# Making ten of the 56 feed-forward gelu tiles straight from PSUM, with a new table of who computes which softmax tile

## The chip, the cores and the metric

The kernel runs on one core of a Trainium2 chip. The metric is device time in microseconds (us) of one execution, the median of several. TensorE is called PE here, VectorE DVE, ScalarE ACT, GpSimd POOL and SyncE SP, as in the profile.

## The reference, cut to what matters

The input `x` is normalised once, and two branches read the result: attention with 32 query heads over one shared key and value head, and a feed-forward layer with a tanh-approximated gelu. The sum of `x` and both is the output.

```python
xn = layernorm(x)                      # x: 1 x 2048 x 512, bfloat16
q = (xn @ wq) as 32 heads of 16;  k = xn @ wk;  v = xn @ wv      # one k and v for all heads
p = softmax(q k^T / 4);  attn = (p v) as 2048 x 512 @ wo
h = gelu(xn @ w1 + b1)                 # w1: 512 x 1792
out = x + attn + h @ w2 + b2
```

## The kernel before, in words

**Softmax tiles.** Scores are computed transposed, keys on the partitions. A tile is 128 keys by 512 queries of one head. There are 2,048 tiles (4 blocks of 512 tokens, 8 groups of 4 heads, 16 key tiles, 4 heads) in 683 units of three. `scores(u)` writes the three tiles of unit `u` into banks 0 to 2 of PSUM when `u` is even and 3 to 5 when it is odd, so a unit's scores can start only once the unit two before it has been read. Bank 6 collects the probability-times-value sums (the pv matmuls), and bank 7 (`pM`, the side bank) serves everything else, one result at a time.

**Two ways for the exponential.** A tile's exponential is computed either by ACT (`exp`, into the buffer `E`, one pv matmul follows) or by DVE with an integer approximation: `p1` reads the bank and writes an int16 tile into `Dt`, `close_batch` makes three shifted copies of it and at last shifts the first tile itself, and five pv matmuls add up the five versions. DVE makes the copies; the last shift, called the in-place step below (line 1139 of the profile), is planned for POOL, but DVE takes it where the planner finds DVE free earlier. The string `DTAB` has one character a unit and says which of its tiles go to DVE: `.` none, `0` or `o` the first, `2` or `t` the third, `a` the first two, `x` or `X` all three (the letters `o t A B X` also close a batch of copies).

**Side work.** Projections of q, the feed-forward tiles and the output are cut into small jobs that are placed at units by tables (`QK`, `HP`, `YP`). `h_mm(tb, ft)` makes one feed-forward tile: 128 of the 1,792 hidden features for the 512 tokens of block `tb`. It issues 16 column-tiled matmuls (`mm4`, four for each quarter of the 512 inputs) into `pM`, and DVE adds the bias `b1T` and writes bfloat16 into `ubs[tb % 2]`: `ub` for the even blocks, and the no longer needed `x_sb` for the odd ones. There are 14 such tiles a block, 56 in all.

**Gelu batches.** Gelu needs another function table on ACT than exp does. So the gelus of two blocks are done together: `GU` places one batch after unit 182 (blocks 0 and 1) and one after unit 512 (blocks 2 and 3). `gelu` issues four activations a batch, each over `FG` = 7 tiles, in place in SBUF. While ACT is at them, DVE works on units whose three tiles are all its own. Later the y jobs multiply the gelu'd tiles by `w2`.

**Order.** `Prog.schedule` is a planner in the kernel: it simulates the five engines with costs written in the code and fixes each engine's order of instructions; `emit` adds the semaphore waits. On PE, scores come first, then the rest by due time. `op.sdeps` are dependencies for the planner, `op.rel` a release mark, and `allow` how long after becoming ready a step may wait.

Of the kernel before, what the change touches and what calls it, by code (L numbers as in the profile page):

```python
# [6 lines left out]
ACT = mybir.ActivationFunctionType  # L7
# [25 lines left out]
EV_ALLOW = -2.0  # L33
# [25 lines left out]
DMASK = {".": (), "0": (0,), "2": (2,), "a": (0, 1), "b": (1, 2), "x": (0, 1, 2),  # L59
         "o": (0,), "t": (2,), "A": (0, 1), "B": (1, 2), "X": (0, 1, 2)}  # L60
CLOSE = "otABX"
DTAB = "000to.2t0000t...t0t0..ooo0.o202t2.t..22t2.2t00.t2.0ot2.22o0002..0.o0o.2t22o2o0.00o.o.t.0o2tt.2.2t2o.2o2.20t0.00t22t.222o.2.2o.02.t2o0o.20ooot2.t0o0.t.o0.0t22t.ot.02oo2.2o.t022t0.2000oxXXXot...ooo2tt.202o0t0.t22t.0t2t.22t2ot.2.0oot2o.000.t0ot.20t.to0t02t0o.ot20oo0.20t2o0o..0o.o20o202.0t2t.2.t00oo..2oo020tt.020.t0o0.2.to.222t20o..t000t.2o.ttt22.2too.t.02ot20.t2.o0t0t2o.o0.t002020o..tt220o0.o2o.2t.22tt.o0.02t0oto0.00t.to2t.2.2tt0002t00o.t00.2t22..2o.00otot..2tt2t.t202..o.00t0.o.02o0.ot0t.2t00.tt2t220.0o00o22.2txXxtottot2o.t00t.2tt.ot22oo.tt.ot0.ooot002.to2o.t22o02.oo0o.2oo2t.220oo000.oo02.t.002o002o20.2t22o2t..2o.tttt0tt.2o.00t0t.0o0200t.t22tt00.2tt0.0o20t.0ttot0.2.ot2t..0o.0.."
YF = 664
Y_ALLOW = 2.0
H_ALLOW = 1.0
# [31 lines left out]
H_PRO = ()  # L97
# [6 lines left out]
TBW = 512  # L104
# [473 lines left out]
def bass_parallel_sum__grouped_kv_mqa__dense_activation_gelu__prompt_kernel(  # L578
# [21 lines left out]
    FT = F // P  # L600
    NTB = S // TBW
# [10 lines left out]
    with ExitStack() as es:  # L612
# [5 lines left out]
        ubs = (ub, x_sb)  # L618
# [15 lines left out]
        b1T = sb([P, FT], f32, "b1T")  # L634
# [51 lines left out]
        pO, pM = bank(6), bank(7)  # L686
        pr = Prog(nc)
# [3 lines left out]
        def B(b):  # L691
            return ("bank", b)
# [6 lines left out]
        def act(fn, r=(), w=(), n=TBW, allow=0.0, lat=0.22, **kw):  # L699
            return add("act", fn, r, w, occ=0.051 + n / 1.2e3, lat=lat, allow=allow, **kw)  # L700
# [17 lines left out]
        M4 = [(("bank", 7), j) for j in range(4)]  # L718
# [28 lines left out]
        def setup(fn, r=(), w=(), occ=0.16, due=0.0, lat=0.1, **kw):  # L747
# [31 lines left out]
              r=["mrow"], w=["isc"], due=10.0)  # L779
# [10 lines left out]
        for gl in range(2):  # L790
# [5 lines left out]
                    n=1500, due=0.01)  # L796
# [70 lines left out]
        def tr(a, b):  # L867
            return [("xnT", ti) for ti in range(a, b)]
# [375 lines left out]
        def ukey(tb, f):  # L1244
            return ("x", f) if tb % 2 else ("u", 0, f)

        def h_mm(tb, ft, ev=EV_ALLOW):
            for d in range(DT):
                mm4(pM, w1_sb[:, d, ft * P:(ft + 1) * P], xnT[:, d, tb * TBW:(tb + 1) * TBW], d == 0, d == DT - 1,
                   r=["w1"] + tr(4 * tb, 4 * tb + 4), w=[B(7)], allow=H_ALLOW if tb < NTB - 1 else 1.5)  # L1250
            dve(lambda e: e.tensor_scalar(ubs[tb % 2][:, ft, :], pM, b1T[:, ft:ft + 1], None, ALU.add),  # L1251
                r=["b1T"], w=M4 + [ukey(tb, ft)], n=TBW + 57, allow=ev)

        gelu_after = {}

        def gelu(tbs, u):
            parts = [(tb, f0) for tb in tbs for f0 in range(0, FT, FG)]
            hold = exps[u - 3:u + 1]
            for n, (tb, f0) in enumerate(parts):
                uu = ubs[tb % 2][:, f0:f0 + FG, :]  # L1260
                uk = [ukey(tb, f) for f in range(f0, min(FT, f0 + FG))]
                load = 1.35 * (n == 0) + 1.35 * (n == len(parts) - 1)
                o = act(lambda e, uu=uu: e.activation(uu, uu, ACT.Gelu_apprx_tanh), r=uk, w=uk, n=len(uk) * TBW + 1200 * load + 40,
                        kind="gelu", due=0.0, after=hold)
# [192 lines left out]
```

## Time and profile before

| | |
|---|---|
| median of 3 runs | 746.38 us (745.35 to 746.84) |
| the profiled execution | 746.57 us, span of its instructions 744.8 us |
| busy | PE 730.0, DVE 731.1, ACT 729.7, POOL 383.1 us |
| ACT, exps | 676 instructions, 680.5 us |
| ACT, gelu batches | 209.7 to 224.7 and 553.1 to 568.2 us, table loads included |
| DVE, h evacuations | 56 of 738 ns |
| granted TensorE clock, mean | 0.998 |

Records of one engine overlap, since an instruction starts before the one ahead has left the engine's pipeline; so sums of durations exceed the time they fill, and the step from one start to the next is the better price. PE's busy time is modelled and tells little. A group's line names the line, the engine, the operation, output and input tiles with their shapes, then busy us, mean ns of one, and the idle time before it with what ended it.

### The profile page before, as it was taken

How to read it: one execution, taken by the hardware profiler on the slowest of the kernel's cores; microseconds unless marked ns; L12 is line 12 of the kernel's file. 1: busy time of each engine (PE TensorE's matmuls, PEld its weight loads, DVE VectorE, ACT ScalarE, POOL GpSimd, SP SyncE). 2: the span in 40 equal slices, each digit the busy share in tenths (PEclk: the TensorE clock that was granted, in tenths of full speed). 3: DMA queues.
4: the chain of work that ended last, by engine and by line, in shares of the span. 5: the costliest groups of instructions: out<-in, count | busy, mean ns of one | idle time of the engine just before them, and what ended most of it. 6: DMA issues, size and time to landing. Idle time of an engine off the chain costs nothing.

```text
span 744.8 us, 22099 instructions
## 1 busy us (share of the span) xinstructions
PE 730.0 (98%) x9040; PEld 215.0 (29%) x9042; DVE 731.1 (98%) x1412; ACT 729.7 (98%) x741; POOL 383.1 (51%) x548
## 2 busy tenths in 40 slices
PE   7999999999999999999999999999998999999998
PEld 4322222222232222222222222222232222222223
DVE  7999999999999999999999999999999999999996
ACT  8899999999999999999999999999999999999995
POOL 7434555545533546545656455343543646546560
PEclk9999999999999999999999999999999999999999
DMA  9200100000011010100101110100100101010011
GB/s 310 66 19 17 30 11 19 22 11 16 16 46 30 13 35 18 24 16 16 32 7 26 26 38 18 37 16 15 24 12 24 31 17 38 16 46 17 10 31 37
DMA packets 31198, 23.34 MB, mean 31 GB/s; under 512 B 16385, under 2 KB 25722, under 8 KB 31098
## 3 DMA queue, kind: packets, MB, share of 16 engines
q1 hardware_dynamic: 31098, 21.94, 11.2%
q8 instruction: 72, 1.18, 0.7%
q14 instruction: 28, 0.23, 0.1%
HBM read 13.08 MB, written 2.35 MB: 21 GB/s over the span
## 4 chain that ended last, share of the span: by engine, by line
ACT 62%; PE 22%; DVE 13%; DMA 1%; SPq 1%; issue 1%
ACT E L1065 62%; PE pAll L1109 10%; PE pAll L1042 6%; DVE Dt L1096 6%; PE pAll L714 5%; DVE Dt L1143 5%; DMA b1row<-in_B_b_dram 1%; SPq L721 1%; DVE Of L1155 1%; PE pAll L708 0%; PE pAll L1418 0%; DVE Dt L1139 0%; DVE x_sb L1251 0%; DVE xnT L864 0%; DVE qp L1223 0%
## 5 line engine op out<-in xcount | busy, mean ns | idle before, releaser
L1065 ACT ACTIVATE E<-pAll 128x1024 bf16<-128x1024 f32 (+1 forms) x676 | 680.5, 1285 | 1.6 <-PE pAll L1042 1.5
L1139 POOL TENSOR_SCALAR Dt<-Dt 128x512 int16<-128x512 int16 x454 | 342.3, 754 | 325.9 <-DVE Dt L1143 116.0
L1109 PE MATMUL pAll<-Dt,V 128*32 128x512 bf16 x2775 | 409.4, 386 | 2.6 <-DVE Of L1155 2.3
L1096 DVE TENSOR_SCALAR Dt<-pAll 128x512 int16<-128x512 f32 (+1 forms) x541 | 367.6, 693 | 1.9 <-PE pAll L1042 1.0
L1109 PE MATMUL pAll<-E,V 128*32 128x512 bf16 x1493 | 303.9, 384 | 0.2 <-DVE Of L1155 0.2
L1143 DVE TENSOR_SCALAR Dt<-Dt 128x1024 int16<-128x1024 int16 (+6 forms) x540 | 288.0, 559 | 0.4
L1042 PE MATMUL pAll<-QT,KT 32*128 32x512 bf16 x2048 | 267.4, 385 | 4.5 <-ACT E L1065 2.4
L1042 PEld LDWEIGHTS pAll<-QT,KT 32*128 32x128 bf16 x2048 | 66.8, 91 | 295.3 <-ACT E L1065 283.8
L1109 PEld LDWEIGHTS pAll<-Dt,V 128*32 128x32 bf16 x2775 | 103.3, 95 | 102.5 <-issue 69.6
L1109 PEld LDWEIGHTS pAll<-E,V 128*32 128x32 bf16 x1493 | 72.9, 95 | 44.0 <-issue 33.0
L714 PE MATMUL pAll<-xnT,w_sb 128*32 128x512 bf16 x896 | 84.9, 384 | 0.0
L714 PE MATMUL pAll<-w_sb,x_sb 128*32 128x512 bf16 x448 | 76.4, 384 | 0.0
L714 PE MATMUL pAll<-w_sb,ub 128*32 128x512 bf16 x448 | 64.3, 383 | 0.1
L714 PE MATMUL pAll<-wop,oTp 128*32 128x512 bf16 x256 | 51.9, 383 | 0.0
L1186 POOL TENSOR_TENSOR oTp<-OfP,rbP 128x256 bf16<-128x256 f32 (+1 forms) x28 | 22.5, 809 | 14.6 <-DVE Dt L1143 7.9
L714 PEld LDWEIGHTS pAll<-xnT,w_sb 128*32 128x32 bf16 x896 | 21.4, 95 | 26.6 <-issue 16.8
L714 PE MATMUL pAll<-xnT,wq_sb 128*32 128x512 bf16 x256 | 26.8, 383 | 0.0
L1139 DVE TENSOR_SCALAR Dt<-Dt 128x512 int16<-128x512 int16 x101 | 26.2, 279 | 0.0
L1155 DVE COPY Of<-pAll 128x512 f32<-128x512 f32 x31 | 21.1, 680 | 0.1
L714 PEld LDWEIGHTS pAll<-w_sb,x_sb 128*32 128x32 bf16 x448 | 18.3, 95 | 8.2 <-issue 6.7
L1251 DVE TENSOR_SCALAR ub<-pAll,b1T 128x512 bf16<-128x512 f32 x28 | 20.7, 738 | 0.0
L1251 DVE TENSOR_SCALAR x_sb<-pAll,b1T 128x512 bf16<-128x512 f32 x28 | 20.7, 738 | 0.0
(125 smaller groups left out, 264.5 us busy)
## 6 DMA issues: line engine op xcount, KB each, us to landing
OfP<-Of SPq DMA_DIRECT2D x124, 32.0 KB, 2.0
rbP<-rden_rows SPq DMA_DIRECT2D x124, 32.0 KB, 1.8
w_sb<-in_B_w_dram SPq DMA_DIRECT2D x2, 1792.0 KB, 11.4
x_sb<-in_A_x_dram SPq DMA_DIRECT2D x18, 128.0 KB, 2.3
QT<-qp SPq DMA_DIRECT2D x124, 16.0 KB, 1.8
x_sb<-in_A_x_dram SPq DMA_DIRECT2D x7, 256.0 KB, 3.9
out_dram<-x_sb SPq DMA_DIRECT2D x12, 128.0 KB, 1.9
wq_sb<-in_A_wq_dram SPq DMA_DIRECT2D x1, 512.0 KB, 5.9
```

Source lines behind the costliest of these rows:

```text
L714: add("pe", lambda e, c=c, j=j: e.matmul(o[c, :], l[:, c], rh, start=start, stop=stop, tile_position=(0, 32 * j)), r, [(k, j) for k in w] ...
L721: return add(eng, lambda e: e.dma_start(o, i), r, w, dma=stream, occ=occ, lat=lat, allow=allow, **kw)
L1042: ins = e.matmul(o, l, rh, start=True, stop=True, tile_position=(q0, 0))
L1065: o = act(lambda e: e.activation(E[:, s0:s0 + na, :], bank(b0, na).rearrange("p (a n) -> p a n", a=na), ACT.Exp, scale=LN2 / 128.0), w=[B( ...
L1096: op = dve(lambda e: e.tensor_scalar(Dt[:, s:s + n, :], bank(bk, n).rearrange("p (a n) -> p a n", a=n), float(127 * 128) + SPL_D, SPL_MIN, ...
L1109: add("pe", lambda e, a, b: e.matmul(pO[32 * j:32 * j + 32, :], V1[:, v, kt, :], rhs, start=a, stop=b, tile_position=(0, 32 * j)), r=r + [ ...
L1139: add("pool", lambda e, d=d, k=k: e.tensor_scalar(d, d, 1.0, float(k), ALU.mult, ALU.add), [], [(("D", base[o > 0] + q), o)], occ=PL_OCC, ...
L1143: dve(lambda e, d=view(o, nb), q=view(i, nb), k=k: e.tensor_scalar(d, q, float(k), None, ALU.add), r=keys(i), w=keys(o), n=nb * n * TBW, m ...
L1155: dve(lambda e: e.tensor_copy(Of[:, i, :], pO), w=["O", ("Of", i)], allow=0.0)
L1186: "pool", lambda e, c=c: e.tensor_tensor(oTp[0:n, sl, c], OfP[0:n, s, c], rbP[0:n, s, c], ALU.mult),
L1251: dve(lambda e: e.tensor_scalar(ubs[tb % 2][:, ft, :], pM, b1T[:, ft:ft + 1], None, ALU.add), r=["b1T"], w=M4 + [ukey(tb, ft)], n=TBW + 57 ...
```

## The change

Of the 14 h tiles of the odd block of each batch, the last five (`GM` = 5, tiles 9 to 13) are no longer made ahead by `h_mm`. They are made during the gelu batch: 16 matmuls into `pM`, and then ACT reads the bank itself, adds the bias as the activation's per-partition bias, applies gelu and writes SBUF. These are called directs below. The other 23 tiles of the batch are done in six parts (`GCH` = 6) of 4, 4, 3, 3, 5 and 4 tiles, and a direct stands between each two parts. `DTAB` is another string, with 554 tiles for DVE instead of 555; `GU`, `HP` and the other tables stay.

```diff
-DTAB = (683 characters)
+DTAB = (683 others)
+GM = 5
+GCH = 6
...
+        def h_proj(tb, ft, al):
             for d in range(DT):
                 mm4(pM, w1_sb[:, d, ft * P:(ft + 1) * P], xnT[:, d, tb * TBW:(tb + 1) * TBW], d == 0, d == DT - 1,
-                   r=["w1"] + tr(4 * tb, 4 * tb + 4), w=[B(7)], allow=H_ALLOW if tb < NTB - 1 else 1.5)
+                   r=["w1"] + tr(4 * tb, 4 * tb + 4), w=[B(7)], allow=al)
+
+        def h_mm(tb, ft, ev=EV_ALLOW):
+            h_proj(tb, ft, H_ALLOW if tb < NTB - 1 else 1.5)
             dve(lambda e: e.tensor_scalar(ubs[tb % 2][:, ft, :], pM, b1T[:, ft:ft + 1], None, ALU.add),
...
         def gelu(tbs, u):
-            parts = [(tb, f0) for tb in tbs for f0 in range(0, FT, FG)]
+            te, to = tbs
+            n0 = round(GCH * FT / (2 * FT - GM)) if GM else 2
+            parts = []
+            for tb, n, k in ((te, FT, n0), (to, FT - GM, (GCH if GM else 4) - n0)):
+                f = 0
+                for i in range(k):
+                    m = -(-(n - f) // (k - i))
+                    parts.append((tb, f, m))
+                    f += m
+            seq = []
+            direct = list(range(FT - GM, FT))
+            for p in parts:
+                seq.append(p)
+                if direct:
+                    seq.append((to, direct.pop(0), 0))
+            seq += [(to, f, 0) for f in direct]
             hold = exps[u - 3:u + 1]
...
+            for n, (tb, f0, m) in enumerate(seq):
+                load = 1.35 * (n == 0) + 1.35 * (n == len(seq) - 1)
+                if m:
+                    uu = ubs[tb % 2][:, f0:f0 + m, :]
+                    uk = [ukey(tb, f) for f in range(f0, f0 + m)]
+                    o = act(lambda e, uu=uu: e.activation(uu, uu, ACT.Gelu_apprx_tanh), r=uk, w=uk, n=m * TBW + 1200 * load + 40,
+                            kind="gelu", due=0.0, after=hold)
+                else:
+                    n0_ = len(pr.ops)
+                    h_proj(tb, f0, H_ALLOW)
+                    for op in pr.ops[n0_:]:
+                        op.sdeps.append((exps[u - 3], True))
+                        op.rel = exps[u - 3]
+                    o = act(lambda e, tb=tb, f0=f0: e.activation(ubs[tb % 2][:, f0, :], pM, ACT.Gelu_apprx_tanh, bias=b1T[:, f0:f0 + 1]),
+                            r=["b1T"], w=M4 + [ukey(tb, f0)], n=TBW + 1200 * load, kind="gelu", due=0.0, after=hold)
                 hold = [o]
...
-                if tb > 0 or ft not in [h[0] for h in H_PRO]:
+                if (tb > 0 or ft not in [h[0] for h in H_PRO]) and not (tb % 2 and ft >= FT - GM):
                     at(HP[tb][ft], lambda tb=tb, ft=ft: h_mm(tb, ft), 0.66)
```

On ACT, at the first batch, the order before was this (`E<-pAll` is an exp, `ub<-ub` and `x_sb<-x_sb` a gelu part):

```order
L1065 ACTIVATE E<-pAll 128x1024 x5
L1263 ACT_TABLE_LOAD
L1263 ACTIVATE ub<-ub 128x3584 x2
L1263 ACTIVATE x_sb<-x_sb 128x3584 x2
L1065 ACT_TABLE_LOAD
L1065 ACTIVATE E<-pAll 128x1024 x2
L1065 ACTIVATE E<-pAll 128x1536 x3
```

And it is now, from the last exp ahead of the batch to the batch's fifth direct (`x_sb<-pAll,b1T`):

```order
L1067 ACTIVATE E<-pAll 128x512
L1284 ACT_TABLE_LOAD
L1284 ACTIVATE ub<-ub 128x2048
L1292 ACTIVATE x_sb<-pAll,b1T 128x512
L1284 ACTIVATE ub<-ub 128x2048
L1292 ACTIVATE x_sb<-pAll,b1T 128x512
L1284 ACTIVATE ub<-ub 128x1536
L1292 ACTIVATE x_sb<-pAll,b1T 128x512
L1284 ACTIVATE ub<-ub 128x1536
L1292 ACTIVATE x_sb<-pAll,b1T 128x512
L1284 ACTIVATE x_sb<-x_sb 128x2560
L1292 ACTIVATE x_sb<-pAll,b1T 128x512
```

Four long activations have become eleven, five of which read a bank that PE fills within the batch.

On PE, in the first batch, the order before was this, with the semaphores that a row waits for (`QT,KT` are scores, `Dt,V` pv matmuls on DVE's tiles, `xnT,w_sb` an h tile, `xnT,zeros` fillers):

```order
L1042 MATMUL pAll<-QT,KT 128x512 [waits tk_dve]
L1042 MATMUL pAll<-QT,KT 128x512 x2
L1109 MATMUL pAll<-Dt,V 32x512 x3
L714 MATMUL pAll<-xnT,w_sb 32x512 [waits tk_dve]
L714 MATMUL pAll<-xnT,w_sb 32x512 x15
L1418 MATMUL pAll<-xnT,zeros 32x512 x12
L1109 MATMUL pAll<-Dt,V 32x512 [waits tk_dve]
L1109 MATMUL pAll<-Dt,V 32x512 x10
```

And it is now, with the matmuls of the second and of the third direct in the first and last two rows:

```order
L716 MATMUL pAll<-xnT,w_sb 32x512 [waits tk_act]
L716 MATMUL pAll<-xnT,w_sb 32x512 x15
L1111 MATMUL pAll<-Dt,V 32x512 [waits tk_dve]
L1111 MATMUL pAll<-Dt,V 32x512 x3
L1447 MATMUL pAll<-xnT,zeros 32x512 x4
L1044 MATMUL pAll<-QT,KT 128x512 [waits tk_dve]
L1044 MATMUL pAll<-QT,KT 128x512 x2
L1111 MATMUL pAll<-Dt,V 32x512 x3
L716 MATMUL pAll<-xnT,w_sb 32x512 [waits tk_act]
L716 MATMUL pAll<-xnT,w_sb 32x512 x15
```

An h tile's matmuls now wait for ACT to have read the bank, and between two of them PE has rows that wait for DVE.

In the whole program, by counting rows of the order: exps 678 for 676 (534 of two tiles for 535, 141 of three as before, 3 of one); pv matmuls on DVE's tiles 2,770 for 2,775; DVE's part of the in-place steps 125 for 101; output normalisations on DVE (line 1186 before) 7 for 4. Behind the batches, ACT's first two exps are those of units 183 and 188 (187 and 188 before), and of 515 and 518 (516 and 517 before).

More of the change, by code (lines that the diff above doesn't have):

```diff
@@ L61 @@
 CLOSE = "otABX"
-DTAB = "000to.2t0000t...t0t0..ooo0.o202t2.t..22t2.2t00.t2.0ot2.22o0002..0.o0o.2t22o2o0.00o.o.t.0o2tt.2.2t2o.2o2.20t0.00t22t.222o.2.2o.02.t2o0o.20ooot2.t0o0.t.o0.0t22t.ot.02oo2.2o.t022t0.2000oxXXXot...ooo2tt.202o0t0.t22t.0t2t.22t2ot.2.0oot2o.000.t0ot.20t.to0t02t0o.ot20oo0.20t2o0o..0o.o20o202.0t2t.2.t00oo..2oo020tt.020.t0o0.2.to.222t20o..t000t.2o.ttt22.2too.t.02ot20.t2.o0t0t2o.o0.t002020o..tt220o0.o2o.2t.22tt.o0.02t0oto0.00t.to2t.2.2tt0002t00o.t00.2t22..2o.00otot..2tt2t.t202..o.00t0.o.02o0.ot0t.2t00.tt2t220.0o00o22.2txXxtottot2o.t00t.2tt.ot22oo.tt.ot0.ooot002.to2o.t22o02.oo0o.2oo2t.220oo000.oo02.t.002o002o20.2t22o2t..2o.tttt0tt.2o.00t0t.0o0200t.t22tt00.2tt0.0o20t.0ttot0.2.ot2t..0o.0.."
+DTAB = "02oto.0o20tt.t..0t0t..to.t022o.02o.o.oo.o.t0o0.22t.00ott22..t2t.00ot00.0t.2o2o2tt2t..t2.20t20.t.2o2o.0022.t.2220t000.tt.2o2.o20.22o.2t.t0t200o0t..o20.o00o2o0.t222022.t.0o20220t202.t.a2xoXoott2o2.0o.t0t.otto2tt2tt22.020t.0o.00oot.2oo..o0t022to22..2.o0t22to0.ot022tot.o022t0..t002o2.0t02tt.220.o.t0.02o2t002..0o0t.20t2t.2o.00t.t0.22t.0t2ot.02o0...t0t0t..ot2tt2o2oo.t2t.2o.o02o220t2t.20.o200oo0.o2..ooo20o..t2o.t2t0oo.2ot22t22.t.2t2202t.too00020200t.2....2tttt0to.o.2t2..t2t2.002o0oo.t2.220.0.tto.02o2t0o22202t002t.oxXaXot.20oo0o.oo2t.2t.22.tB.2ototoo0t2.t0220...tt02o200tt.t.o2.o22t2o.2t0t0222o0t..t20o2.2to00to0.o22t2..tt20o22.tt2t.0o22o2.t22.tt22t2ot.too00..o.oto.2t0o0o2t.o.ot.t0..."
 YF = 664
@@ L1245, in ukey @@
             return ("x", f) if tb % 2 else ("u", 0, f)
-        def h_mm(tb, ft, ev=EV_ALLOW):
+        def h_proj(tb, ft, al):
             for d in range(DT):
                 mm4(pM, w1_sb[:, d, ft * P:(ft + 1) * P], xnT[:, d, tb * TBW:(tb + 1) * TBW], d == 0, d == DT - 1,
-                   r=["w1"] + tr(4 * tb, 4 * tb + 4), w=[B(7)], allow=H_ALLOW if tb < NTB - 1 else 1.5)
+                   r=["w1"] + tr(4 * tb, 4 * tb + 4), w=[B(7)], allow=al)
+        def h_mm(tb, ft, ev=EV_ALLOW):
+            h_proj(tb, ft, H_ALLOW if tb < NTB - 1 else 1.5)
             dve(lambda e: e.tensor_scalar(ubs[tb % 2][:, ft, :], pM, b1T[:, ft:ft + 1], None, ALU.add),
@@ L1256, in gelu @@
         def gelu(tbs, u):
-            parts = [(tb, f0) for tb in tbs for f0 in range(0, FT, FG)]
-            hold = exps[u - 3:u + 1]
[L1259 to L1264, printed above, removed]
+            te, to = tbs
[14 more added lines that the diff above has]
+            seq += [(to, f, 0) for f in direct]
+            hold = exps[u - 3:u + 1]
+            for n, (tb, f0, m) in enumerate(seq):
[13 more added lines that the diff above has]
+                            r=["b1T"], w=M4 + [ukey(tb, f0)], n=TBW + 1200 * load, kind="gelu", due=0.0, after=hold)
                 hold = [o]
```

## The prediction

> **What bounds the kernel now.** I read first the page's span and busy times, then a table of stages that I cut at the two gelu batches, then the list of waits.
>
> ```profile
> span 744.8 us, 22099 instructions
> PE 730.0 (98%) x9040; PEld 215.0 (29%) x9042; DVE 731.1 (98%) x1412; ACT 729.7 (98%) x741; POOL 383.1 (51%) x548
> ```
>
> Three engines read 98%, so the shares alone say nothing. The table of stages (the columns are PE, PEld, DVE, ACT, POOL busy with instruction counts, then TensorE clock) separates them:
>
> ```profile
> 24.00:209.00 185.00, 183.14 (x2223) 52.05 (x2220) 184.21 (x338) 185.00 (x183) 96.42 (x132) 1.00 0.08 18
> 209.00:228.00 19.00, 18.85 (x257) 7.05 (x259) 18.96 (x26) 18.62 (x10) 6.03 (x9) 1.00 0.17 45
> 228.00:551.00 323.00, 321.47 (x4018) 90.78 (x4014) 322.34 (x626) 323.00 (x322) 166.33 (x218) 1.00 0.09 23
> 551.00:573.00 22.00, 19.13 (x228) 7.03 (x220) 21.51 (x32) 20.90 (x13) 9.29 (x14) 0.92 0.07 16
> 573.00:735.00 162.00, 160.96 (x2072) 44.45 (x2064) 160.65 (x332) 162.00 (x164) 90.00 (x114) 1.00 0.11 25
> ```
>
> In the three long stages ACT is busy for all of 185, 323 and 162 us: it never stops. It falls short only in the two short stages that hold the batches, by 0.38 and 1.10 us. The waits say who waits for whom:
>
> ```profile
> PEld pAll L1042 <- ACT E L1065: 283.8, 656, 0.8
> PEld pAll L1042 <- DVE Dt L1096: 8.0, 18, 0.7
> ACT E L1065 <- PE pAll L1042: 1.5, 3, 1.0
> ```
>
> The scores of a unit wait for ACT's exp 656 times of 683, for DVE's part 18 times; ACT waits for scores three times. ACT sets the pace, so what counts is work put on ACT, and gaps between its instructions.
>
> How full is ACT inside those stages? Its records overlap, so I need start-to-start steps. These are the two exp forms and the gelu parts, then one clean run of ten exps (one of 3 tiles, then nine of 2), then ACT around the batches:
>
> ```profile
> L1065 ACT ACTIVATE E<-pAll 128x1024 bf16<-128x1024 f32 x535 | 527.0, 1197 | 1.2 <-PE pAll L1042 1.2
> L1065 ACT ACTIVATE E<-pAll 128x1536 bf16<-128x1536 f32 x141 | 224.0, 1619 | 0.3 <-PE pAll L1042 0.3
> L1263 ACT ACTIVATE ub<-ub 128x3584 bf16<-128x3584 bf16 x4 | 12.5, 3182 | 0.0
> L1065 ACT ACTIVATE E<-pAll x10: 1041/1101/1454, 283.5 to 292.0; 128x1024 bf16<-128x1024 f32 x9, 128x1536 bf16<-128x1536 f32 x1
> ...
> 209.67 1.28 ACT L1263 ACT_TABLE_LOAD   x1
> 210.97 6.27 ACT L1263 ACTIVATE ub<-ub 128x3584 bf16<-128x3584 bf16 x2
> 217.15 6.25 ACT L1263 ACTIVATE x_sb<-x_sb 128x3584 bf16<-128x3584 bf16 x2
> 223.42 1.28 ACT L1065 ACT_TABLE_LOAD   x1
> 224.71 1.94 ACT L1065 ACTIVATE E<-pAll 128x1024 bf16<-128x1024 f32 x2
> 226.97 8.72 ACT L1065 ACTIVATE E<-pAll 128x1536 bf16<-128x1536 f32 x8 [0.32 <-PE pAll L1042]
> ...
> 571.11 9.86 ACT L1065 ACTIVATE E<-pAll 128x1024 bf16<-128x1024 f32 x10 [0.99 <-PE pAll L1042]
> ```
>
> One tile more costs 1.619 - 1.197 = 0.422 us. The nine steps from 283.5 to 292.0 hold 3 + 8 x 2 = 19 tiles: 8.5 = 19 x 0.422 + 9e, so an exp's fixed part e is 0.054 us. A gelu part of 7 tiles steps (217.15 - 210.97) / 2 = 3.09 us, a fixed part of 3.09 - 7 x 0.422 = 0.136. All exps then need 1,493 x 0.422 + 676 x 0.054 = 667 us. The long stages hold 183 + 322 + 164 = 669 exps in 670 us, against some 660 of need: about 10 us, or 1.5%, of small gaps are spread between the exps. That and the batches' gaps are all that a faster partner of ACT could give back.
>
> **The change, part by part.**
>
> *DVE loses ten evacuations.* Each is a step of 0.67 us (216.01 to 216.68), 6.7 us in all:
>
> ```profile
> L1251 DVE TENSOR_SCALAR x_sb<-pAll,b1T 128x512 bf16<-128x512 f32 x28 | 20.7, 738 | 0.0
> 216.01 0.75 DVE L1251 TENSOR_SCALAR x_sb<-pAll,b1T 128x512 bf16<-128x512 f32 x1
> 216.68 0.95 DVE L1143 TENSOR_SCALAR Dt<-Dt 128x3072 int16<-128x3072 int16 x1
> ```
>
> DVE is not what ACT waits for, so I book nothing. Nor does the new table turn the time into tiles taken off ACT: it has 554 tiles on DVE for 555. What fills DVE instead are in-place steps that POOL did: 125 of them on DVE for 101, at (0.88 - 0.28) / 3 = 0.20 us a step, 4.8 us in all.
>
> ```profile
> L1139 DVE TENSOR_SCALAR Dt<-Dt 128x512 int16<-128x512 int16 x101 | 26.2, 279 | 0.0
> 230.03 0.88 DVE L1139 TENSOR_SCALAR Dt<-Dt 128x512 int16<-128x512 int16 x4
> ```
>
> *ACT's exps.* One tile more (1,494), in 678 instructions for 676 (534 of two tiles, 141 of three, 3 of one): 0.422 + 2 x 0.054 = +0.53 us, on the path.
>
> *ACT's gelus.* The 56 tiles stay the same, so their elements cost the same. Twelve parts from SBUF stand for eight: 4 x 0.136 = +0.54. Ten directs are new, each with a fixed part of its own. No row shows a gelu from PSUM. The nearest are ACT's two PSUM reads of 128x512, one with a bias per partition, one without:
>
> ```profile
> L882 ACT ACTIVATE KT<-pAll,krow 128x512 bf16<-128x512 f32 x1 | 0.7, 687 | 0.9 <-DVE krow L982 0.9
> L911 ACT ACTIVATE QT<-pAll 128x512 bf16<-128x512 f32 x1 | 0.6, 572 | 0.0
> ```
>
> The bias costs 687 - 572 = 115 ns. So the fixed part lies between 0.054 (as the exp, without bias) and 0.169 (exp plus bias); I take 0.169, since the direct has that bias: +1.69, at least +0.54. Work on ACT: 0.53 + 0.54 + 1.69 = +2.8 us, at least +1.6. A hidden cost it isn't: ACT never stops.
>
> The Trainium skill's ScalarE: Activation LUTs, What ACT_TABLE_LOAD costs, speaks against the directs too: each `[128,1]` pointer operand adds about 93 ns to an ACTIVATE. By that the ten directs add an estimated 1.47 us and the work is +2.5; the row above says 115 ns, and the sum goes by the row.
>
> *New waits: ACT for PE, ten times.* A direct needs 16 matmuls just made in the side bank, and these must wait until the direct before has read it. The same 16 stand in the trace:
>
> ```profile
> 214.15 1.05 PE L714 MATMUL pAll<-xnT,w_sb 128*32 128x512 bf16 x16
> ...
> 226.53 0.39 PE L1042 MATMUL pAll<-QT,KT 32*128 32x512 bf16 x3
> ```
>
> From one direct's start to the next's readiness: 0.69 (its record, as L882) + 1.05 = 1.74 us and two hops between the engines, 0.05 each (these scores end at 226.92, the exp above starts at 226.97): 1.84. ACT needs for its own direct and a part of three tiles 0.59 + 3 x 0.422 + 0.136 = 1.99, of four 2.41, of five 2.84. So the matmuls hide, just, if PE is free when the bank is. It is not always: in the order, pv matmuls that wait for DVE or POOL, and scores that wait for DVE, stand ahead of the h matmuls on PE. Such waits were short before:
>
> ```profile
> PEld pAll L1109 <- DVE Dt L1143: 2.8, 10, 0.6
> PEld pAll L1109 <- POOL Dt L1139: 4.3, 18, 0.4
> ```
>
> That is 0.3 and 0.2 us on average. Behind a part of three tiles there is room for 0.15: four such places (two a batch) with two short waits each come 0.2 late, and the first direct of batch one, whose matmuls stand behind DVE's mT evacuation, at 0.2: +1.0 us. Bounds: 0, and ten at 0.6, +6. Queued behind ACT's wait are the rest of the gelus and every later exp. The ten h tiles' matmuls are the same 160, only moved, and an h tile issues no DMA; the side work and its DMAs behind them shift by up to a batch, which I cost at nothing, because scores wait on ACT 656 times and not on side work.
>
> *The gaps after the batches.* ACT idled 0.32 and 0.99 us for its third exp, behind crowded PE queues. Now units 183 and 188 are ready at the end of batch one, and 515 and 518 at that of batch two. The third scores then need only the first of these exps to end, if PE has emptied its queue. I take back most: -1.0 (bounds -1.3 and 0). The second gap follows a starved PE (columns as above):
>
> ```profile
> 562.80:566.20 3.40, 1.05 (x17) 0.25 (x11) 3.40 (x8) 3.40 (x2) 0.00 (x0) 0.90 0.02 5
> 566.20:569.60 3.40, 3.40 (x40) 1.49 (x34) 3.40 (x6) 3.37 (x4) 0.00 (x0) 0.60 0.12 31
> ```
>
> With 17 matmuls in 3.4 us the clock in the next 3.4 us is 0.60. The Trainium skill's TensorE: Matmul & The Clock Gate, Part 1, says the same: an idle window of about 3.4 us puts the array at half clock for the next. The rows agree; by that rule the gap goes only if h matmuls break the idle stretch, otherwise 0.99 stays.
>
> *Sum.* +2.8 + 1.0 - 1.0 = +2.8 us. The profiled execution took 746.57 us (span 744.8 and 1.8 around it), 0.19 over the median of 746.38: 746.38 + 2.8 = 749.2. Since the two lower bounds (work +1.6, gaps -1.3) are nearer than the upper, I shade it to **748.9**.
>
> **Rivals.** 0.2% is 1.5 us here, about what a measurement of this kernel can tell from no change.
> 1. *As summed*: ACT's extra work shows. 748 to 750.5. Chance 0.50.
> 2. *The directs starve* (slower still): PE's queue is held by pv matmuls waiting for DVE before most h matmuls, 0.5 a direct, and the gaps stay. 2.8 + 5 = +7.8 at most; 751 to 754. For it: the order, where nearly every h group follows a DVE wait. Against: such waits averaged 0.3. It decides from 0.2 us of lateness. Chance 0.12.
> 3. *DVE's relief counts* (faster): the scattered 10 us of gaps come from scores that wait for a DVE late by one evacuation, 8.0 us in the list. If half go, -4 on top of work at its lower end, +1.6, no new waits, gaps -1.3: -3.7, 742.7; with a quarter, 744.7. It needs at least 1.8 us of the 8.0. For it: ten evacuations fewer at 98% busy. Against: DVE is filled again by in-place steps, and the evacuations touch only the stretches ahead of the batches. Chance 0.13.
> 4. *A draw*: the change doesn't relieve what it says, but costs little: +1.6 - 1.3 + 0.5 = +0.8; 745.5 to 747.8. Chance 0.25.
>
> **The numbers.** The likeliest case gives 748.9. The range leaves out most of rival 3 and the far part of rival 2: 745.0 to 751.8. Faster by over 0.2%: 0.13, within: 0.25, slower: 0.62.
>
> **What would show it.** In the changed profile: ACT's gelu stretch, table load to table load, before 209.67 to 223.42, longer by 1.0 to 1.6 us in each batch; directs of about 0.69 us a record; ACT's idle for PE in the list of waits, by line of the direct, 1 us in total (rival 2: over 3); the exp stages still full. DVE's busy time unchanged within 3 us. The prediction is wrong if the long stages hold their exps at under 0.99 us each for 1.00 now (rival 3), or if the batches grow by over 3 us each.

## The result, and the profile after

The changed kernel takes 749.73 us (median of 5 runs, 749.42 to 750.00) against 746.38: ratio 1.0045, 95% interval 1.0033 to 1.0057, or 3.4 us more. It is slower, by under half a per cent but clear of the noise. Its profiled span is 747.7 us against 744.8, so the trace holds 2.9 of these 3.4 us. Of 77 executions of the kernel before that were timed beside the experiments, 32 had a mean granted clock of 1.000 and a median of 745.58 us and 45 had 0.995 to 0.998 and 746.71 us, while all five of the changed kernel had 1.000, so at the same clock the change costs about 4 us.

The page's span and busy times, and the two stretches of the table of stages that hold the batches (PE, PEld, DVE, ACT, POOL busy with counts, TensorE clock, DMA share, GB/s):

```profile
span 747.7 us, 22053 instructions
PE 734.6 (98%) x9030; PEld 220.7 (30%) x9030; DVE 730.7 (98%) x1445; ACT 732.6 (98%) x757; POOL 362.7 (49%) x520
209.00:228.00 19.00, 18.20 (x263) 10.21 (x258) 15.86 (x32) 18.46 (x16) 2.00 (x4) 1.00 0.13 23
553.00:575.00 22.00, 20.91 (x250) 8.27 (x247) 22.00 (x36) 21.36 (x20) 8.81 (x12) 1.00 0.09 19
```

DVE lost ten evacuations and is as busy as before (730.7 for 731.1): it took in-place steps from POOL (125 for 101, POOL is busy 362.7 for 383.1 us), and in the first batch it stands idle for 3.14 of 19 us, where it stood idle for 0.04. The groups by line, operation and shape, then the list of waits:

```profile
L1292 ACT ACTIVATE x_sb<-pAll,b1T 128x512 bf16<-128x512 f32 x10 | 6.8, 680 | 0.5 <-PE pAll L716 0.4
L1141 DVE TENSOR_SCALAR Dt<-Dt 128x512 int16<-128x512 int16 x125 | 32.4, 284 | 0.2 <-PE pAll L1111 0.2
```

```profile
PEld pAll L1044 <- ACT E L1067: 280.9, 652, 0.8
PEld pAll L1044 <- DVE Dt L1098: 9.8, 23, 0.6
DVE Dt L1098 <- PE pAll L1044: 3.5, 3, 3.1
```

A direct's record is 680 ns. Scores still wait mostly for ACT, and DVE has one new long wait, 3.1 us. Now ACT's timeline at batch one, then the start and the end of batch two:

```profile
208.50 1.28 ACT L1284 ACT_TABLE_LOAD   x1
209.80 1.91 ACT L1284 ACTIVATE ub<-ub 128x2048 bf16<-128x2048 bf16 x1
211.61 0.67 ACT L1292 ACTIVATE x_sb<-pAll,b1T 128x512 bf16<-128x512 f32 x1
212.18 1.90 ACT L1284 ACTIVATE ub<-ub 128x2048 bf16<-128x2048 bf16 x1
...
218.49 0.69 ACT L1292 ACTIVATE x_sb<-pAll,b1T 128x512 bf16<-128x512 f32 x1 [0.43 <-PE pAll L716]
219.07 2.33 ACT L1284 ACTIVATE x_sb<-x_sb 128x2560 bf16<-128x2560 bf16 x1
221.30 0.68 ACT L1292 ACTIVATE x_sb<-pAll,b1T 128x512 bf16<-128x512 f32 x1
221.87 1.91 ACT L1284 ACTIVATE x_sb<-x_sb 128x2048 bf16<-128x2048 bf16 x1
223.80 1.28 ACT L1067 ACT_TABLE_LOAD   x1
225.10 3.02 ACT L1067 ACTIVATE E<-pAll 128x1024 bf16<-128x1024 f32 x3
```

```profile
554.87 1.28 ACT L1284 ACT_TABLE_LOAD   x1
...
569.76 1.28 ACT L1067 ACT_TABLE_LOAD   x1
571.05 1.51 ACT L1067 ACTIVATE E<-pAll 128x512 bf16<-128x512 f32 x2
573.04 3.28 ACT L1067 ACTIVATE E<-pAll 128x1024 bf16<-128x1024 f32 x3 [0.48 <-PE pAll L1044]
```

From the first table load to the first exp behind it, batch one takes 225.10 - 208.50 = 16.60 us and batch two 571.05 - 554.87 = 16.18, against 15.04 each before: +1.56 and +1.14, together **+2.70 us**. A direct steps 212.18 - 211.61 = 0.57, so its fixed part is 0.57 - 0.422 = 0.15. A part of four tiles steps 1.81 and one of five 2.23: a fixed part of 0.12. One direct shows a wait, 0.43 us. The gap after batch one is gone (0.32 before), that after batch two is 0.48 (0.99 before; the part on the prediction says what that 0.99 hangs on).

Outside the batches: before, the first exps start at 23.88 and the last broadcast on ACT at 738.22; now it is this (the rows at both ends of ACT's exps, after and then before):

```profile
23.57 2.85 ACT L1067 ACTIVATE E<-pAll 128x1024 bf16<-128x1024 f32 x3 [0.16 <-PE pAll L1044]
...
741.08 0.41 ACT L1210 ACTIVATE rbP<-rT 128x256 f32<-128x256 f32 x1 [2.38 <-DVE rT L1202]
```

```profile
23.88 2.85 ACT L1065 ACTIVATE E<-pAll 128x1024 bf16<-128x1024 f32 x3 [0.16 <-PE pAll L1042]
...
738.22 0.41 ACT L1208 ACTIVATE rbP<-rT 128x256 f32<-128x256 f32 x1 [2.36 <-DVE rT L1200]
```

The head is 0.31 us shorter, which is scatter: in the nine kernels below made from the kernel before and edited only behind it, the first exp starts between 23.68 and 24.64 us. The three stretches of exps, from these rows and the batches' ends, take 184.93 + 329.77 + 170.03 = 684.73 us, before 185.79 + 328.43 + 170.04 = 684.26: +0.47, about the price of the one tile more. But they contain the gaps after the batches, which shrank by 0.83. So the small gaps between exps grew by about as much (0.47 + 0.83 - 0.53 = 0.77). Where they lie is open. Sum: -0.31 + 2.70 + 0.47 = +2.86, the span's growth.

Where DVE's new hole comes from shows in PE's and then DVE's timeline at the end of batch one:

```profile
219.42 1.08 PE L716 MATMUL pAll<-xnT,w_sb 128*32 128x512 bf16 x15
220.28 2.34 PE L1111 MATMUL pAll<-Dt,V 128*32 128x512 bf16 x19
222.34 2.32 PE L716 MATMUL pAll<-w_sb,ub 128*32 128x512 bf16 x37
...
225.59 1.03 PE L716 MATMUL pAll<-wop,oTp 128*32 128x512 bf16 x13
...
226.66 0.39 PE L1044 MATMUL pAll<-QT,KT 32*128 32x512 bf16 x3
```

```profile
227.10 0.69 DVE L1098 TENSOR_SCALAR Dt<-pAll 128x512 int16<-128x512 f32 x1 [3.11 <-PE pAll L1044]
```

Behind the last direct's matmuls PE works without a break for 6.4 us at pv and side work, and only then come scores, for which DVE has waited 3.11 us.

### The profile page after: what moved, and what is told of

Its sections match the earlier page's. It is cut to its first block, busy times and chain, and to the rows that moved or that the text cites. A ratio compares the mean times of both kernels' runs of the same rounds, so it can differ in the third digit from the quotient of the medians.

```text
span 747.7 us, 22053 instructions
## 1 busy us (share of the span) xinstructions
PE 734.6 (98%) x9030; PEld 220.7 (30%) x9030; DVE 730.7 (98%) x1445; ACT 732.6 (98%) x757; POOL 362.7 (49%) x520
## 4 chain that ended last, share of the span: by engine, by line
ACT 79%; PE 15%; DVE 4%; DMA 1%; SPq 1%; issue 0%; DVEq 0%
ACT E L1067 78%; PE pAll L1111 7%; PE pAll L1044 4%; PE pAll L716 3%; DVE Dt L1098 2%; DMA b1row<-in_B_b_dram 1%; DVE Dt L1145 1%; SPq L723 1%; PE pAll L710 0%; DVE xnT L866 0%; DVE Of L1157 0%; PE pAll L1444 0%; PE pAll L1213 0%; DVE QT L921 0%; DVE qp L1225 0%
## 5 line engine op out<-in xcount | busy, mean ns | idle before, releaser
L1141 POOL TENSOR_SCALAR Dt<-Dt 128x512 int16<-128x512 int16 x429 | 324.0, 755 | 352.9 <-DVE Dt L1145 141.1
L1111 PE MATMUL pAll<-Dt,V 128*32 128x512 bf16 x2770 | 396.9, 383 | 2.1 <-DVE Of L1157 1.3
L1111 PE MATMUL pAll<-E,V 128*32 128x512 bf16 x1494 | 297.7, 384 | 0.0
L1145 DVE TENSOR_SCALAR Dt<-Dt 128x1024 int16<-128x1024 int16 (+7 forms) x556 | 290.8, 550 | 0.3
L716 PE MATMUL pAll<-w_sb,x_sb 128*32 128x512 bf16 x448 | 68.2, 383 | 0.0
L716 PE MATMUL pAll<-w_sb,ub 128*32 128x512 bf16 x448 | 59.5, 383 | 0.0
L716 PE MATMUL pAll<-wop,oTp 128*32 128x512 bf16 x256 | 57.2, 383 | 0.0
L1141 DVE TENSOR_SCALAR Dt<-Dt 128x512 int16<-128x512 int16 x125 | 32.4, 284 | 0.2 <-PE pAll L1111 0.2
L1188 POOL TENSOR_TENSOR oTp<-OfP,rbP 128x256 bf16<-128x256 f32 x25 | 20.3, 821 | 11.0 <-DVE Dt L1145 4.8
L716 PEld LDWEIGHTS pAll<-w_sb,ub 128*32 128x32 bf16 x448 | 16.1, 95 | 10.6 <-issue 7.5
```

The costliest lines, as they stand in the source:

```text
L716: add("pe", lambda e, c=c, j=j: e.matmul(o[c, :], l[:, c], rh, start=start, stop=stop, tile_position=(0, 32 * j)), r, [(k, j) for k in w] ...
L1111: add("pe", lambda e, a, b: e.matmul(pO[32 * j:32 * j + 32, :], V1[:, v, kt, :], rhs, start=a, stop=b, tile_position=(0, 32 * j)), r=r + [ ...
L1141: add("pool", lambda e, d=d, k=k: e.tensor_scalar(d, d, 1.0, float(k), ALU.mult, ALU.add), [], [(("D", base[o > 0] + q), o)], occ=PL_OCC, ...
L1145: dve(lambda e, d=view(o, nb), q=view(i, nb), k=k: e.tensor_scalar(d, q, float(k), None, ALU.add), r=keys(i), w=keys(o), n=nb * n * TBW, m ...
L1188: "pool", lambda e, c=c: e.tensor_tensor(oTp[0:n, sl, c], OfP[0:n, s, c], rbP[0:n, s, c], ALU.mult),
```

## Experiments

The prediction's theory, called A here: ACT alone sets the pace; work on ACT is paid one for one and DVE's relief brings nothing. The rival, B: DVE (or PE) sets it as well. Each kernel was timed against the kernel before on the same chip; us are the ratio's excess times 746.4.

**DVE relieved, kernel before.** The ten evacuations that the change removes are cut short.

```diff
-            dve(lambda e: e.tensor_scalar(ubs[tb % 2][:, ft, :], pM, b1T[:, ft:ft + 1], None, ALU.add),
+            cw = 64 if tb % 2 and ft >= 9 else TBW
+            dve(lambda e: e.tensor_scalar(ubs[tb % 2][:, ft, 0:cw], pM[:, 0:cw], b1T[:, ft:ft + 1], None, ALU.add),
```

> The kernel before, same order of instructions on every engine, but the ten DVE evacuations that the change takes away (h tiles 9 to 13 of the odd blocks) copy only the first 64 of 512 columns, so 448 columns of these tiles are left out. DVE loses about 10 x 0.47 = 4.7 us of the change's 6.7, ACT's work stays. Theory (ACT sets the pace, DVE's relief is worth nothing): 746.4 us, within 0.8 of before. Rival (DVE's relief is worth its time and the change loses it again elsewhere): about 741.7, at least 744 if half counts.

745.73 us, ratio 0.9997 (0.9988 to 1.0006). 4.7 us less of DVE bring nothing that can be told from none, at most 0.9 us.

**DVE loaded, kernel before.** The same ten evacuations are made twice, the first into a dummy.

```diff
+                if tb % 2 and ft >= 9:
+                    e.tensor_scalar(dum[:, ft % 2, :], pM, b1T[:, ft:ft + 1], None, ALU.add)
                 return e.tensor_scalar(ubs[tb % 2][:, ft, :], pM, b1T[:, ft:ft + 1], None, ALU.add)
```

> The kernel before, same order, but the same ten DVE evacuations are each made twice (the first copy goes to a scratch tile): +10 x 0.67 = +6.7 us on DVE, nothing on ACT. Theory (ACT sets the pace; gaps between DVE's work and ACT's are about 10 us over the whole span, but only a few tenths at any one place): small growth, 746.5 to 749. Rival (DVE at 98% is an equal bound): +6 us or more, about 752.5 to 753.

752.25 us, ratio 1.0081 (1.0068 to 1.0095): +6.0 us for about 6.7 us of DVE. All four executions had a clock under 1.000; against the ten such ones of the kernel before on that chip (746.70) it is +5.5. The group shows the ten, and ACT now idles after the first batch:

```profile
L1254 DVE TENSOR_SCALAR dum<-pAll,b1T 128x512 bf16<-128x512 f32 x10 | 7.4, 739 | 0.0
...
229.57 2.79 ACT L1066 ACTIVATE E<-pAll 128x1536 bf16<-128x1536 f32 x2 [1.04 <-PE pAll L1043]
```

Theory A fails here: work put on DVE is paid for the most part, though taking work off it gives nothing. One thing this run doesn't separate: the second evacuation also holds the side bank 0.67 us longer, and PE's weight loads for h tiles wait 5.3 us for the evacuations into `x_sb` (1.2 before).

**ACT relieved, and ACT loaded, kernel before.** In ten units between 100 and 169 the exps take half their columns; in another kernel the same ten units get one exp of a tile more.

```diff
+                cw = 256 if u in (100, 107, 114, 123, 131, 138, 145, 154, 162, 169) else TBW
-                o = act(lambda e: e.activation(E[:, s0:s0 + na, :], bank(b0, na)...,
+                o = act(lambda e: e.activation(E[:, s0:s0 + na, 0:cw], bank(b0, na)...[:, :, 0:cw],
```

> The kernel before, same order, but ten exps of two tiles between units 100 and 169 compute only the first 256 of each tile's 512 columns, the rest is left out: ACT loses 10 x 0.43 = 4.3 us in the stretch ahead of the first batch, DVE and PE lose nothing. Theory A (ACT alone sets the pace): the time falls by most of it, to 742.0 to 743. Theory B (ACT and DVE are bounds side by side, so that relief of one alone is worth little, as the cut of DVE's evacuations to 64 columns was worth 0.5 us or less): 745 to 746.3.

746.07 us, ratio 1.0001 (0.9992 to 1.0010): 4.3 us less on ACT, and nothing that can be told from none comes back.

```diff
+                    if u in (100, 107, 114, 123, 131, 138, 145, 154, 162, 169):
+                        e.activation(dum[:, u % 2, :], bank(b0), ACT.Exp, scale=LN2 / 128.0)
```

> The kernel before, same order, but at the same ten units ACT also computes one tile's exp a second time into a scratch tile: +10 x 0.48 = +4.8 us on ACT ahead of the first batch, nothing elsewhere. In a batch 2.2 us of added ACT work cost 1.0 us. Theory (outside a batch there are no gaps that would take it up): +4 to +4.8, 750.2 to 751. Rival (gaps take up half of it here as well): +1 to +2.5, 747.2 to 748.7.

751.25 us, ratio 1.0067 (1.0054 to 1.0081): +5.0 us for about 4.8. So ACT behaves as DVE does: what is added is paid, what is taken away isn't given back. That is B: DVE and ACT are bounds side by side, and there may be more. (The extra exp, too, holds its bank longer.)

**Both relieved, kernel before.** If the two are the whole bound, relief of both must pay. In one kernel both lie at the same ten units (the first edit below beside the halved exps), in a second the halved exps go with the shortened evacuations, in a third the first also has shorter filler matmuls, and in a fourth the first has shorter scores in 20 units.

```diff
+            cw = 64 if ds[0][0] // 3 in (100, 107, 114, 123, 131, 138, 145, 154, 162, 169) else TBW
-            op = dve(lambda e: e.tensor_scalar(Dt[:, s:s + n, :], bank(bk, n)...,
+            op = dve(lambda e: e.tensor_scalar(Dt[:, s:s + n, 0:cw], bank(bk, n)...[:, :, 0:cw],
...
-            pr.filler = lambda e, j, o: e.matmul((pO if o else pM)[32 * j:32 * j + 32, :], zeros[:, 0:32], xnT[:, 0, 0:TBW],
+            pr.filler = lambda e, j, o: e.matmul((pO if o else pM)[32 * j:32 * j + 32, 0:64], zeros[:, 0:32], xnT[:, 0, 0:64],
...
+                cw = 64 if u in (100, 103, 107, 110, ...) else TBW
-                pieces.append((bank(3 * x + i), KT[...], QT[q0:q0 + 32, g, :], q0))
+                pieces.append((bank(3 * x + i)[:, 0:cw], KT[...], QT[q0:q0 + 32, g, 0:cw], q0))
```

> The kernel before, with ACT and DVE relieved in the same ten units (100, 107, 114, 123, 131, 138, 145, 154, 162, 169): the exps of these units compute 256 of 512 columns, and the DVE tile of the same unit reads 64 of 512 columns (part of the softmax is left out). ACT loses about 4.3 us and DVE about 10 x 0.467 = 4.7 us. If ACT and DVE are joint bounds, and either alone therefore gave back nothing, relief of both at one place gives back 2 to 4 us. If a third engine, PE in its fixed order, holds the pace as well, the time stays within 0.7 us of before.

> The kernel before, with the same ten exps cut to 256 columns (ACT -4.3 us) and the ten DVE h evacuations that the change removes cut to 64 columns (DVE -4.7 us): the relief lies on both engines but mostly at different units. If joint bounds have to be relieved at the same place, under 0.7 us comes back; if the sums of each engine count, 2 to 4 us.

> As the kernel with ACT and DVE relieved in the same ten units, and besides all 124 filler matmuls of PE (zeros into a bank, 13.3 us of records) take 64 of 512 columns. If PE in its fixed order is a third bound, this gives back 2 to 4 us where the one without it gave nothing; if ACT and DVE alone are the bound, it gives the same as that one. A lower granted clock from an idler PE would make it slower.

> As the kernel with ACT (-4.3 us) and DVE (-4.7 us) relieved in the same ten units, and besides the scores of 20 units (those ten and the third after each) compute 64 of 512 columns (part of the scores is left out): by the records a score group's step of 0.32 us falls by about 0.2, so PE loses about 4 us of real work in the same stretch. If PE's real work is the third bound, this goes 1.5 us or more below the kernel with two engines relieved (745.55); if PE is not a bound, it is within 0.7 us of it.

| relieved | us | ratio (95%) | change, us |
|---|---|---|---|
| ACT and DVE, same units | 745.55 | 0.9982 (0.9974 to 0.9991) | -1.3 |
| ACT and DVE, other units | 744.92 | 0.9978 (0.9969 to 0.9988) | -1.6 |
| as the first, fillers cut | 745.08 | 0.9981 (0.9972 to 0.9990) | -1.4 |
| as the first, scores cut | 744.42 | 0.9974 (0.9963 to 0.9985) | -1.9 |

Relief of both does pay, where either alone did not, but only 1.3 to 1.6 us of over 4, less than the 2 that the expectation asked for; place makes no difference that shows, and neither do fillers. The ten units run between 125 and 195 us. The window from 100 to 190 us, which holds nine of them, shows where the rest stays: the kernel before, the one with both relieved at the same units, and the one with scores cut as well:

```profile
100.00:190.00 90.00, 89.30 (x1104) 25.24 (x1096) 89.68 (x165) 90.00 (x90) 47.42 (x67) 1.00 0.07 16
```

```profile
100.00:190.00 90.00, 89.42 (x1118) 25.29 (x1110) 87.79 (x166) 88.64 (x91) 49.15 (x66) 1.00 0.07 16
```

```profile
100.00:190.00 90.00, 88.59 (x1133) 26.08 (x1124) 88.43 (x168) 89.56 (x92) 49.64 (x67) 1.00 0.07 16
```

With both relieved, DVE and ACT go idle (2.2 and 1.4 us of 90) while PE stays at 89.4. With the scores cut too, ACT is again busy for 89.6 us. That speaks for PE's own order as a third bound, but it isn't shown: the expectation asked for 1.5 us below 745.55 if PE is the bound and for under 0.7 if it isn't, and the time lies 1.1 below by the medians and 0.6 by the ratios, whose intervals overlap.

**The directs without bias, changed kernel.**

```diff
-                    o = act(lambda e, tb=tb, f0=f0: e.activation(ubs[tb % 2][:, f0, :], pM, ACT.Gelu_apprx_tanh, bias=b1T[:, f0:f0 + 1]),
+                    o = act(lambda e, tb=tb, f0=f0: e.activation(ubs[tb % 2][:, f0, :], pM, ACT.Gelu_apprx_tanh),
```

> The changed kernel, same order, but the ten directs leave out the bias b1. Theory (the fixed part of a direct on ACT is paid in full by the time): a direct's record falls from 680 ns to about 570, its step from 0.57 to about 0.47, and the time by 10 x 0.1 = 1.0 us, from 749.7 to about 748.7. Rival (the loss is in waits for PE and stalls around the batch, not in ACT's own work): the steps shrink but ACT waits longer for PE, 749.5 or more.

749.37 us, ratio 1.0043 (1.0030 to 1.0057) for 1.0045. The group of directs, then the first table load, the start of one direct and of the part behind it, and the exps behind batch one:

```profile
L1292 ACT ACTIVATE x_sb<-pAll 128x512 bf16<-128x512 f32 x10 | 5.9, 590 | 0.9 <-PE pAll L716 0.8
...
208.49 1.28 ACT L1284 ACT_TABLE_LOAD   x1
...
211.60 0.58 ACT L1292 ACTIVATE x_sb<-pAll 128x512 bf16<-128x512 f32 x1
212.07 1.90 ACT L1284 ACTIVATE ub<-ub 128x2048 bf16<-128x2048 bf16 x1
...
227.08 6.04 ACT L1067 ACTIVATE E<-pAll 128x1024 bf16<-128x1024 f32 x6 [0.25 <-PE pAll L1044]
```

A step of 0.47 for 0.57: 1.0 us less on ACT in ten, but the time falls by no more than a difference that can't be told from none. The wait for PE at the directs doubles, 0.4 to 0.8 us, and behind the batch ACT waits again, 0.25 us.

**The directs cut to 64 columns, changed kernel.**

```diff
-                    o = act(lambda e, tb=tb, f0=f0: e.activation(ubs[tb % 2][:, f0, :], pM, ACT.Gelu_apprx_tanh, bias=b1T[:, f0:f0 + 1]),
+                    o = act(lambda e, tb=tb, f0=f0: e.activation(ubs[tb % 2][:, f0, 0:64], pM[:, 0:64], ACT.Gelu_apprx_tanh, bias=b1T[:, f0:f0 + 1]),
```

> The changed kernel, same order, but each of the ten directs reads and writes only 64 of 512 columns, 448 are left out: ACT loses 10 x 0.37 = 3.7 us inside the two batches. Theory A (a batch lasts as long as ACT's work in it): 746.0. Theory B (PE's matmuls behind DVE and POOL, and DVE's own work, end hardly earlier than ACT; leaving out the bias took 1.0 us from ACT and 0.4 us from the time): ACT waits for PE at most directs and again for the scores behind the batch, 748 to 749.

749.75 us, ratio 1.0050 (1.0037 to 1.0062): 3.7 us less on ACT, and nothing comes back, less even than the 748 to 749 that the expectation gave for B. ACT's timeline, and then PE's at the end of batch one:

```profile
208.75 1.28 ACT L1284 ACT_TABLE_LOAD   x1
...
216.24 0.32 ACT L1292 ACTIVATE x_sb<-pAll,b1T 128x64 bf16<-128x64 f32 x1 [0.59 <-PE pAll L1111]
...
218.73 0.31 ACT L1292 ACTIVATE x_sb<-pAll,b1T 128x64 bf16<-128x64 f32 x1 [0.80 <-PE pAll L716]
...
227.34 6.04 ACT L1067 ACTIVATE E<-pAll 128x1024 bf16<-128x1024 f32 x6 [0.81 <-PE pAll L1044]
```

```profile
219.66 1.08 PE L716 MATMUL pAll<-xnT,w_sb 128*32 128x512 bf16 x15
...
226.90 0.39 PE L1044 MATMUL pAll<-QT,KT 32*128 32x512 bf16 x3
```

From the last direct's matmuls to the first scores PE takes 226.90 - 219.66 = 7.24 us, as with whole directs (226.66 - 219.42 = 7.24). In this kernel the end of the batch is PE's; in the changed kernel the scores end at 226.66 + 0.39 = 227.05, and ACT's two exps from 225.10 on, at about 0.96 a step, at 227.0: both chains end together.

The third exp behind a batch shows it best, since it is the first one that waits for scores made behind the batch's work on PE. Counted from the batch's first table load, it starts after 227.34 - 208.75 = 18.59 us here, after 227.08 - 208.49 = 18.59 without the bias, and after 18.59 in the changed kernel, for batch one; for batch two it is 573.04 - 554.87 = 18.17 in the changed kernel and 18.17 in the other two. In the kernel before it is 226.97 - 209.67 = 17.30 and 17.96, in batch two with two tiles more of exps ahead of it. So the directs' length on ACT, whole, without bias or cut to 64 columns, doesn't move the end of a batch: PE's order of work, with its short waits for DVE, sets it. That PE is later than before because each batch now also holds five h tiles' matmuls, 1.05 us each, is likely, but no run shows it by itself.

**ACT's extra work without the directs, kernel before.** The eight gelu parts are issued as 32 instructions of two or one tiles.

```diff
+                    for f in range(0, FG, 2):
+                        v = uu[:, f:min(f + 2, FG), :]
+                        ins = e.activation(v, v, ACT.Gelu_apprx_tanh)
```

> The kernel before, same order, but each of the eight gelu parts of 7 tiles is issued as four activations of 2, 2, 2 and 1 tiles: 24 instructions more on ACT, each with a fixed part of 0.10 to 0.136 us, no tile and no wait more. Theory (work added to ACT in a batch is paid one for one): +2.4 to +3.3 us, 748.8 to 749.7, as much as the whole change. Rival (a batch has slack, because PE and DVE are behind when it ends): under +1 us.

747.25 us, ratio 1.0014 (1.0005 to 1.0023): +1.0 us. ACT at batch one:

```profile
210.06 1.28 ACT L1266 ACT_TABLE_LOAD   x1
211.36 6.83 ACT L1266 ACTIVATE ub<-ub 128x1024 bf16<-128x1024 bf16 x8
218.09 6.82 ACT L1266 ACTIVATE x_sb<-x_sb 128x1024 bf16<-128x1024 bf16 x8
224.93 1.28 ACT L1065 ACT_TABLE_LOAD   x1
226.22 5.97 ACT L1065 ACTIVATE E<-pAll 128x1024 bf16<-128x1024 f32 x5
```

The batch takes 16.16 us for 15.04, and the gap behind it is gone; batch two does the same, and no gap is left behind it. 2 x 1.12 - (0.32 + 0.99) = 0.93, about the +1.0. So in the kernel before work added to ACT in a batch is paid once it has filled the gap, the room in which it costs nothing. The room behind batch two is 1.0 us only where the clock falls there: among executions with a mean clock below 1.000 this kernel costs 0.55 us (747.25 for 746.70), among those with 1.000 it costs 1.65 (747.32 for 745.67).

**The changed code with the table of before.**

```diff
-DTAB = (683 characters)
+DTAB = (the 683 of the kernel before)
```

> The changed code with the table of the kernel before: ten evacuations are gone from DVE, the batches have directs, and nothing was fitted to it. Theory (the batch's form costs about 2.7 us on ACT, and the table is fitted to one exact order, so that stalls are added wherever the order shifts): clearly slower than 749.7, 755 to 770, with idle time of ACT in the list of waits. Rival (the new table is what costs, the directs are harmless): 746 to 749.

761.26 us, ratio 1.0205 (1.0191 to 1.0219). The first direct waits 3 us, and exps elsewhere 9.4 us for pv matmuls:

```profile
ACT E L1067 <- PE pAll L1111: 9.4, 8, 2.7
ACT x_sb L1292 <- PE pAll L716: 3.0, 1, 3.0
```

So the table is fitted to one exact order: with the new one, the changed code is 11 to 12 us faster than with the old one. The two halves of the change can't be priced apart by this, and the code of before with the new table was not run.

## Why the prediction was right, and which of its reasons were not

**The time** came as summed: +2.8 forecast and shaded to 748.9; the span grew by 2.86, the median is 749.73. That the sum met the span this closely is in good part luck, as the terms show. Nearly all the signs that the prediction named came as well (the batches from load to load 1.55 and 1.14 us longer, directs of 0.68 us, full exp stages, DVE's busy time unchanged), but they would have come under theory B too, so they didn't test the reason.

**ACT's work.** The term of the exps, +0.53, can't be seen by itself; their stretches grew by 0.47. As prices the others were good: the four more gelu parts take 4 x 0.12 = 0.49 us of ACT for 0.54, the ten directs' fixed parts 10 x 0.15 = 1.5 for 1.69. But the prediction put them on the path ("A hidden cost it isn't: ACT never stops"), and for the directs that failed: with 1.0 or 3.7 us less of them both batches end where they ended. What the sum books as the directs' time is, in the runs, the later end of PE's order. The bias, read off two unlike rows as 115 ns, is 90 ns by records that differ in nothing else. The Trainium skill's ScalarE: Activation LUTs, What ACT_TABLE_LOAD costs, gives about 93 ns for such an operand; the 90 ns agree with it better than the row that was used.

**New waits** were put at 1.0. The batches grew by 2.70, of which 0.49 + 1.5 is ACT's work: 0.7 is left, 0.43 in one visible wait, at the fourth direct of batch one, behind a part of three tiles. Rival 2, that the directs starve, did not come true at its size.

**Gaps after the batches**: -1.0 forecast, -0.83 measured. But this step was only half seen. Small gaps elsewhere grew by 0.77 for a reason that stays open, and in the sum they cancel this term; the head's scatter of -0.31 and the smaller waits and fixed parts made up for that. The clock in the stretch of batch two is 1.00 now (0.92 before), and none of six stretches of 3.4 us from 554.8 us on holds fewer than 36 matmuls, where one held 17: h matmuls break PE's idle stretch there. That agrees with the Trainium skill's TensorE: Matmul & The Clock Gate, Part 1. The 0.99 itself was not a fixed part of the kernel before. The kernel with halved exps is not edited near batch two, and its profiled execution has the same idle stretch, but no lower clock behind it and no gap over 0.10 us:

```profile
562.40:565.80 3.40, 1.06 (x22) 0.34 (x17) 3.40 (x9) 3.40 (x2) 0.00 (x0) 1.00 0.02 6
565.80:569.20 3.40, 3.31 (x46) 1.36 (x34) 3.40 (x5) 3.37 (x4) 0.00 (x0) 1.00 0.12 31
```

So an idle stretch of this length lowers the clock in some executions only, and the change takes the gap away only from those; against the others its 0.48 us is more, not less.

**DVE's relief at nothing.** The value was right: shortening the ten evacuations alone brought nothing that shows. DVE's busy time stayed (730.7 for 731.1), mostly with 24 more in-place steps and more copies in place of the evacuations. Rival 3 needed at least 1.8 us from this relief; the run leaves room for 0.9 at most, for 4.7 of the 6.7 us.

**The step that failed is the reason given**: "ACT sets the pace, so what counts is work put on ACT". The row behind it, 656 waits of scores for ACT against 18 for DVE, is true, and it does not mean that. 6.7 us added to DVE cost 6.0, and 4.3 us taken from ACT brought nothing. A wait is put down to whoever came last; of two chains that end almost together the list shows one. Another line of the page of the kernel before hinted at it, the chain that ended last by its shares of the span:

```profile
ACT 62%; PE 22%; DVE 13%; DMA 1%; SPq 1%; issue 1%
```

A third of it runs over PE and DVE. The 10 us of small gaps in the exps' stretches may have been a sign of it; the prediction read them only as what a faster partner could give back.

So the change loses like this. Its saving lies on one of at least two bounds side by side, and by itself is worth nothing. In the batches it puts work on ACT and on PE, and the batches end later, at the time that PE's order sets. One tile more for ACT and the small gaps, 0.53 and 0.77 us, are the rest of the trace's growth but for the head, and no run tests these two. What it could bring to let DVE take tiles from ACT in the evacuations' place is argued, not shown: a tile costs DVE about 0.68 (the record of its bank read) and copies and a last shift on top, so 6.7 us are at most ten tiles, ten times 0.422 or 4.2 us of ACT, and nearer six with these steps, 2.5 us, against the 2.7 that the batches grew by. Open stays why the new table gives DVE one tile less instead, where the small gaps come from, and whether PE is a third bound outside the batches. None of the kernels that do the whole computation was faster than the one before.

## What to carry to other kernels

When several engines read 98% in a fixed order, test each from both sides before calling one the bound: add a few us to it and take a few off. Here what was added to an engine, mostly outside the batches, was paid at some 80% or more, and every relief of one engine was worth nothing that shows, so a trade between engines in such a kernel is best priced with its costs in full and its savings at zero, unless a run shows otherwise. A count of waits names who came last, not by how much.

## What the runs showed of the hardware

Gelu straight from PSUM costs ACT no more per element than from SBUF: the directs' records are 680 ns with 512 columns and 309 with 64, so (680 - 309) / 448 = 0.83 ns an element; from SBUF a part of five tiles steps 2.23 - 1.81 = 0.42 us more than one of four, 0.82 ns an element. It costs less to start: without bias a direct steps 0.47 us, 0.05 over its 512 elements at 0.422 us, while a part from SBUF starts for 0.12 by its step, and the pieces of two tiles for 1.12 / 12 = 0.093 each. The Trainium skill's Perfetto Trace Analysis, Optimizing Scalar/DVE Operations, states such an overhead of about 51 ns on PSUM and 93 ns on SBUF; the direct and the pieces agree with it, the longer parts lie a little above. The per-partition bias adds 0.10 to the step (0.57 for 0.47), so with it a direct's start, 0.15, is the dearer one, as the prediction had it.

An idle stretch of TensorE of about 3.4 us, with 17 to 22 matmuls in it, was followed by a lower clock in one execution (0.60 in the next 3.4 us) and by a full clock in another (1.00). Executions of the kernel before with the lower mean clock took 1.1 us more than those with 1.000, so differences of this size are best read between executions of the same clock.
